# Attention and experts on one core: the choice on the tile count turned round, the small last tile in two banks, the gate products behind the first second product

## The chip, the cores and the metric

The kernel runs on one core of one Trainium2 chip. The metric is the device time of one execution in microseconds (us), as the median of several runs. Engines are named as in the profile: PE (TensorE products), PEld (its weight loads), DVE (VectorE), ACT (ScalarE), POOL (GpSimd), SP (SyncE, which issues most of the transfers).

## What is computed

Causal attention over 4 batches, 12 heads, 448 rows and a head width of 64 gives 1792 tokens of width 768. Each token then goes to one of 8 experts, the one with the largest cosine logit, and the expert's output is scaled by the gate:

```python
logits = xn @ en.T / tau
expert_idx = np.argmax(logits, axis=1)
gate_w = probs[np.arange(N), expert_idx]
for e in range(E):
    mask = expert_idx == e
    h = np.maximum(x[mask] @ w1[e], 0.0)
    out[mask] = gate_w[mask, None] * (h @ w2[e])
```

How many tokens an expert gets is only known on the chip.

## The kernel before

The first part is the attention. A list written out by hand (`ORDER`, lines 39 to 107) sets the order of its steps on every engine; it also holds the first expert tile (tile 0) up to most of its second product. The tokens are sorted by expert into tiles of at most 128 rows, each tile for one expert. With eight experts there are 13 to 21 tiles (`NT` is 21, `TMIN` is 14); the number is read from the chip into a register `nt` (line 1060). In the profiled execution there are 18 tiles, 0 to 17.

`body(t)` (line 969) does one tile: the first product of tile t (`product1`), the copies of its result by ACT (`hiddens`), the turning of the next tile's tokens (`turn_x`, line 631, transposes on PE), the gather of tile t+3 by POOL (line 568), then `turned_h` (line 742), which runs the second product of tile t-1 with the transposes of tile t's hidden values put among it, then `split_h` and `finish(t - 1)`: ACT scales the left half by the gate (line 797), DVE the right half (line 800), and POOL writes the rows out with an indirect transfer (line 818). Splitting the next weights into a high and a low part (`split_w`, lines 966 and 967) and loading the ones after them (`loads`, line 954) stand in between. `last(t)` (line 1003) does the second product of the very last tile and its `finish`.

Every product exists in several forms, of which a branch on the chip takes one per tile (`either`, `branch`, lines 580 to 607): *whole* for up to 128 rows (three products for each step of the sum, lines 705 to 707), *small* for up to 64 rows (two, lines 714 and 715) and, from tile 14 on, *tiny* for up to 32 rows (`tiny_product`, line 717). `tiny_product` puts four quarters of the columns on four groups of 32 partitions, all in the accumulator `acc[0]`; in `finish` ACT then scales quarters 0 and 1 (line 809) and DVE quarters 2 and 3 (line 810). Tile 17 is tiny.

Tiles 1 to 13 always exist. From tile 14 on, `rest(t)` (line 1066) chooses on `nt`. The code is nested: behind the choice comes the code of `body(t)`, then all that follows it, and only behind everything the code of `last(t - 1)`. So the code of `last(17)` stands behind that of tiles 18, 19 and 20, which this execution does not run.

```python
with tc.If(nt > t) as c:
    body(t)
    rest(t + 1)
hs[t - 1] = keep
with c.Else():
    last(t - 1)
```

The gate of each token is found by DVE, ACT and POOL (`gate_parts`, lines 1010 to 1035) while PE works on tile 1. `gates()` (line 1048) then brings the gates into the order of the tiles with 16 products on PE and three small operations on DVE; it stands in `body(1)` ahead of `turned_h`. `upper()` (line 1037, in `body(2)`) moves the gates to other partitions with products and two DVE copies, for the small and tiny forms.

PSUM has eight banks. In this part banks 0 and 1 hold the first product (`acc1`, and the second product of the last tile), banks 6 and 7 the second product (`acc2`), and banks 2 to 5 go round in `pt_ring` for transposes and gates.

Each engine runs its own instructions in the order of the code; which one waits for which is set by semaphores.

Of the kernel before, what the change touches and what calls it, by code (L numbers as in the profile page):

```python
# [20 lines left out]
DM, E, F = 768, 8, 1024  # L21
# [7 lines left out]
KD, KF = DM // P, F // P  # L29
# [5 lines left out]
QR = 32  # L35
NQ = P // QR
# [94 lines left out]
def attn_moe(tc, qk, vv, emb, tau, w1, w2, out):  # L131

    nc = tc.nc
    v, g, ac, pe, sy = nc.vector, nc.gpsimd, nc.scalar, nc.tensor, nc.sync
    with ExitStack() as ctx:
# [7 lines left out]
        def T(name, shape, d=F32, parts=CP):  # L143
            return kp.tile([parts] + shape, d, name=name)

        def cut(a, parts, *dims, at=0):

            n = 1
            for d in dims:
                n *= d  # L150
            a = a[:parts, at : at + n]
            if len(dims) == 1:
                return a
            names = "abcd"[: len(dims)]
            return a.rearrange(f"p ({' '.join(names)}) -> p {' '.join(names)}", **dict(zip(names, dims)))
# [59 lines left out]
        r2, xt0, r1 = cut(fa, P, KF, DM), cut(fa, P, DM, at=W), cut(fa, P, KD, F, at=W + DM)  # L215
        at = 2 * W + DM
        hh1, obs, xt1, hh0 = (cut(fa, P, n, at=at + o) for n, o in ((F, 0), (DM, F), (DM, F + DM), (F, F + 2 * DM)))
# [13 lines left out]
        xt_ring = Ring(xt0, xt1)  # L231
# [51 lines left out]
        gt, gu, gq = T("gt", [NT], parts=P), T("gu", [NT], parts=P), T("gq", [NT], parts=P)  # L283
        hq, xq = T("hq", [KF, QR], parts=P), en.rearrange("p k r -> p k r")
# [279 lines left out]
        xs, hs, hb = {}, {}, {}  # L564
# [37 lines left out]
        def either(t, engine, small_, whole_, light_=None, tiny_=None):  # L602

            if t < 2:
                whole_()
            else:
                branch(few[t][engine], small_, whole_, light_, tiny_ if t >= TMIN else None)
# [109 lines left out]
        def tiny_product(acc, x, w, nk, n):  # L717

            for k in range(nk):
                for q in range(NQ):  # L720
                    pe.matmul(acc[0][QR * q : QR * q + QR, :n], x[:, k], w[:, k, n * q : n * q + n], start=k == 0,
                              stop=k == nk - 1, tile_position=(0, QR * q), skip_group_check=True)

        few = [None] * NT

        def product1(t, acc):
            either(t, ET.PE, lambda: small_product(acc, xs[t][1], h1, l1, range(KD), KD, 512),
                   lambda: product(acc, *xs[t][1:], h1, l1, range(KD), (0, KD - 1), 512),
                   tiny_=lambda: tiny_product(acc, xq, r1, KD, F // NQ))

        def product2(t, acc):
            def small_():
# [9 lines left out]
        def turned_h(t, acc, ks):  # L742


            pf[t] = [cut(pt_ring.next(), P, 4, P) for a in range(2)]
            hs[t] = (hb[t], th_ring.next(), tl_ring.next())

            n = 3 if t > 1 else 1

            def among(f):  # L750
                f(ks[:-n])
                turn_h(t)
                f(ks[-n:])

            def whole_(k):
                product(acc, *hs[t - 1][1:], h2, l2, k, (K0[0], K0[-1]) if t == 1 else (0, KF - 1), 384)

            either(t - 1, ET.PE, lambda: among(lambda k: small_product(acc, hs[t - 1][1], h2, l2, k, KF, 384)),
                   lambda: among(whole_))
# [19 lines left out]
        acc2 = [bo[:, :384], bx[:, :384]]  # L779

        def finish(t, acc, ends):
            ob = xt_ring.next() if ends else obs

            def half(j):
                return ob[:, 384 * j : 384 * j + 384]

            def low(j):
                return hb[t][0:64, 384 * j : 384 * j + 384]

            def small_a(j):  # L790
                ac.activation(low(j), acc[j][64:128], AF.Copy, scale=gu[64:128, t : t + 1])

            def small_v(j):
                v.scalar_tensor_tensor(half(j)[0:64], acc[j][0:64], gt[0:64, t : t + 1], low(j), op0=ALU.mult, op1=ALU.add)

            def whole_a():
                ac.activation(half(0), acc[0], AF.Copy, scale=gt[:, t : t + 1])

            def whole_v():
                v.tensor_scalar(half(1), acc[1], gt[:, t : t + 1], None, ALU.mult)  # L800

            def quarters(qs, f):
                n = DM // NQ
                for q in qs:
                    rows = slice(QR * q, QR * q + QR)
                    f(ob[0:QR, n * q : n * q + n], acc[0][rows, :n], gq[rows, t : t + 1])

            def tiny_():
                quarters((0, 1), lambda o, x, s: ac.activation(o, x, AF.Copy, scale=s))
                quarters((2, 3), lambda o, x, s: v.tensor_scalar(o, x, s, None, ALU.mult))  # L810

            if ends and t > 1:
                branch(load_few(t, [ET.DVE, ET.Activation]), lambda: [f(j) for j in range(2) for f in (small_a, small_v)],
                       lambda: (whole_a(), whole_v()), tiny_=tiny_ if t >= TMIN else None)
            else:
                either(t, ET.Activation, lambda: [small_a(j) for j in range(2)], whole_a)
                either(t, ET.DVE, lambda: [small_v(j) for j in range(2)], whole_v)
            g.indirect_dma_start(out=out, out_offset=IndirectOffsetOnAxis(ap=isx[:, t : t + 1], axis=0), in_=ob,  # L818
                                 in_offset=None, bounds_check=N - 1, oob_is_err=False)
# [121 lines left out]
        for token in ORDER.split():  # L941
            name, p = token.split(".")
            pairs, f = steps[name]
# [24 lines left out]

        def body(t):
            product1(t, acc1)  # L970
            if t == 2:
                upper()
            elif t == 1:
                hidden(t, acc1, 0)
                hidden(t, acc1, 1)
            if t + 1 < NT:
                with tc.If(cc[t + 1] == 1):  # L977
                    split_w(r1, h1, l1, range(KD))
                loads(t + 2, 1)
            if t > 1:  # L980
                hiddens(t, acc1)
            if t + 1 < NT:
                few[t + 1] = {e: load_few(t + 1, [e]) for e in (ET.PE, ET.DVE, ET.Activation)}
            if t + 1 < NT:
                next_x(t + 1, turn_x(t + 1))
            if t + 3 < NT:
                gather(t + 3)
            if t == 1:
                gates()
            turn_light(t)  # L990
            ks = K0[GE:] if t == 1 else list(range(KF))
            turned_h(t, acc2, ks)
            if t > 1:
                with tc.If(cc[t] == 1):  # L994
                    split_w(r2, h2, l2, range(6))
            split_h(t)
            finish(t - 1, acc2, False)
            if t > 1:
                with tc.If(cc[t] == 1):  # L999
                    split_w(r2, h2, l2, range(6, KF))  # L1000
            loads(t + 1, 2)

        def last(t):
            acc = [a[:, :384] for a in acc1]
            product2(t, acc)
            finish(t, acc, True)
# [30 lines left out]
        def upper():  # L1037

            b = pt_ring.next()
            f, fq = b[:, :NT], b[:, NT : 2 * NT]  # L1040
            pe.matmul(f[64:128], idt[:, 0:64], gt, start=True, stop=True, tile_position=(0, 64), skip_group_check=True)
            v.tensor_copy(gu[64:128], f[64:128])
            for q in range(NQ):
                pe.matmul(fq[QR * q : QR * q + QR], idt[:, 0:QR], gt, start=True, stop=True, tile_position=(0, QR * q),
                          skip_group_check=True)
            v.tensor_copy(gq, fq)

        def gates():
            tg = cut(pt_ring.next(), P, 3, NT)
            for c in range(NCH):  # L1050
                pe.matmul(tg, M1[:, c], Mg[:, c], start=c == 0, stop=c == NCH - 1)
            v.tensor_copy(gt, tg[:, 2])
            v.scalar_tensor_tensor(gt, gt, 2.0 ** -12, tg[:, 1], op0=ALU.mult, op1=ALU.add)
            v.scalar_tensor_tensor(gt, gt, 2.0 ** -12, tg[:, 0], op0=ALU.mult, op1=ALU.add)
# [5 lines left out]
        nt = val(2 * NT, NT, [ET.SP, ET.Activation, ET.DVE, ET.PE, ET.Pool])  # L1060
        for t in range(1, TMIN):
            body(t)
            if t == 1:
                loads(2, 2)

        def rest(t):
            if t == NT:
                last(NT - 1)
                return
            keep = hs[t - 1]  # L1070
            with tc.If(nt > t) as c:  # L1071
                body(t)
                rest(t + 1)
            hs[t - 1] = keep
            with c.Else():
                last(t - 1)

        rest(TMIN)

# [34 lines left out]
```

## Time and profile before

| | |
|---|---|
| median of 3 runs | 505.75 us (505.46 to 508.03) |
| the profiled execution, its own time | 504.5 us |
| span of the profiled execution, first to last instruction | 502.7 us |
| busy: PE, DVE, ACT, POOL | 96%, 66%, 64%, 14% of the span |
| instruction transfers | 41 of 0.67 MB together on queue 8, 50 of 0.41 MB on queue 14 |
| weight transfers in all | 72.38 MB on queue 1 |

Times in the views are counted from the first instruction of the span. A matmul's start is measured, its end is modelled, so the next one may begin before the end that is shown. A row of a timeline gives start, duration, engine, line, operation, output and inputs, and in brackets how long the engine had been idle and what ended that. A q behind an engine (PEldq) is its sequencer: it reads the code, takes branches, and fills the engine's queue ahead of the engine. Queue 8 carries the code of PE, queue 14 that of the other engines.

### The profile page before, as it was taken

What the parts mean: (1) busy time and instruction counts of PE and PEld (TensorE: products, weight loads), DVE (VectorE), ACT (ScalarE), POOL (GpSimd) and SP (SyncE); (2) the same over time, 40 slices, a digit from 0 to 9 for tenths busy, and PEclk for the clock granted to TensorE, in tenths of its full rate; (3) what the DMA queues carried; (4) which work ended last, traced back from release to release, by engine and by line L of the source; (5) the groups of instructions that cost most, each with busy time, mean ns of one, the idle gap of its engine ahead of it and who ended that gap; (6) DMA issues with size and microseconds to landing.
All of it is one profiled execution on the core that took longest, in us unless ns stands there. A gap on an engine that the chain in (4) does not pass through costs nothing. (4 is left out here: it accounts for less than half of the span.)

```text
span 502.7 us, 10651 instructions
## 1 busy us (share of the span) xinstructions
PE 484.6 (96%) x3180; PEld 384.1 (76%) x3180; DVE 334.0 (66%) x939; ACT 323.9 (64%) x795; POOL 69.7 (14%) x89
## 2 busy tenths in 40 slices
PE   8999999999999998999999999999999999999992
PEld 5656566666666566888899888999889889888981
DVE  4766585766758659862577886873989367478431
ACT  5999999999999994641135965354938352161530
POOL 2000000000000262221002121111202210110111
PEclk9999999999999999999999999999999999999998
DMA  8232453173136862312167871649577701827871
GB/s 257 62 107 82 132 173 111 57 217 113 57 101 196 319 236 90 95 32 64 57 260 289 341 262 68 249 151 398 185 282 288 250 34 33 309 94 279 308 264 37
DMA packets 27371, 87.23 MB, mean 174 GB/s; under 512 B 2694, under 2 KB 3142, under 8 KB 27280
## 3 DMA queue, kind: packets, MB, share of 16 engines
q1 hardware_dynamic: 24160, 72.38, 41.3%
q0 software_dynamic: 3120, 13.77, 7.5%
q8 instruction: 41, 0.67, 0.6%
q14 instruction: 50, 0.41, 0.2%
HBM read 144.33 MB, written 12.58 MB: 312 GB/s over the span
## 5 line engine op out<-in xcount | busy, mean ns | idle before, releaser
L383 ACT ACTIVATE aq<-aq,mx 112x112 f32<-112x112 f32 (+3 forms) x192 | 99.8, 525 | 4.1 <-DVE mx L378 4.1
L378 DVE CUSTOM_DVE_ANT_0 aq<-bank,ar 112x112 f32<-112x112 f32 (+1 forms) x192 | 76.1, 442 | 30.2 <-PE bank L373 29.9
L401 PE MATMUL bank<-idt,aq 112*112 112x112 f32 x480 | 62.5, 266 | 1.2 <-DVE ap L406 0.5
L401 PEld LDWEIGHTS bank<-idt,aq 112*112 112x112 f32 x480 | 46.6, 133 | 19.8 <-ACT ap L406 6.8
L373 PE MATMUL bank<-ak 64*112 64x112 f32 (+3 forms) x384 | 56.2, 416 | 1.0 <-DVE mx L378 0.8
L764 ACT COPY fa<-bank 128x512 f32<-128x512 f32 x28 | 15.2, 588 | 59.9 <-PE bank L705 41.9
L406 ACT COPY ap<-bank 112x336 f32<-112x336 f32 (+2 forms) x118 | 50.7, 458 | 3.4 <-PE bank L401 1.8
L414 PE MATMUL bank<-ap 112*64 112x448 f32 (+3 forms) x384 | 51.7, 407 | 0.0
L663 DVE STREAM_TRANSPOSE turned<-fa 32x256 f32<-32x256 f32 x112 | 48.8, 436 | 1.5
L818 POOL DMA_INDIRECT out_dram<-fa,isx x18 | 24.1, 1341 | 180.7 <-DVEq L999 55.8
L414 PEld LDWEIGHTS bank<-ap 112*64 112x64 f32 x384 | 25.0, 136 | 30.0 <-issue 18.6
L967 DVE TENSOR_TENSOR wl<-fa,wh 128x1024 fp32r<-128x1024 f32 x36 | 41.5, 1220 | 3.1 <-PE bank L706 1.6
L966 ACT CAST wh<-fa 128x1024 fp32r<-128x1024 f32 x36 | 34.9, 1047 | 3.5 <-PE bank L707 1.6
L383 ACT ACTIVATION_READ_ACCUMULATOR aq<-aq,mx 112x1 f32 x192 | 37.1, 193 | 0.0
L373 PEld LDWEIGHTS bank<-ak 64*112 64x112 f32 x384 | 27.0, 173 | 13.0 <-issue 3.1
L568 POOL DMA_INDIRECT fa<-xd,ig x21 | 23.2, 1104 | 75.3 <-PE bank L636 52.9
L705 PE MATMUL bank<-wh,akr 128*128 128x512 f32 x84 | 32.9, 391 | 0.0
L707 PE MATMUL bank<-wh,akr 128*128 128x512 f32 x84 | 32.9, 391 | 0.0
L707 PE MATMUL bank<-wh,apr 128*128 128x512 f32 x84 | 32.9, 391 | 0.0
L706 PE MATMUL bank<-wl,akr 128*128 128x512 f32 x84 | 32.8, 390 | 0.0
L706 PE MATMUL bank<-wl,aor 128*128 128x512 f32 x84 | 32.8, 390 | 0.0
L705 PE MATMUL bank<-wh,aor 128*128 128x512 f32 x84 | 32.8, 390 | 0.0
(311 smaller groups left out, 1023.3 us busy)
## 6 DMA issues: line engine op xcount, KB each, us to landing
fa<-in_w_dram SPq DMA_DIRECT2D x76, 768.0 KB
fa<-in_w_dram SPq DMA_DIRECT2D x54, 1024.0 KB
ak<-in_qk_dram SPq DMA_DIRECT2D x24, 448.0 KB
ap<-in_vv_dram SPq DMA_DIRECT2D x24, 224.0 KB
xd<-fa SPq DMA_DIRECT2D x3, 1344.0 KB
fa<-in_w_dram SPq DMA_DIRECT2D x6, 512.0 KB
xd<-fa SPq DMA_DIRECT2D x1, 1120.0 KB
fa<-xd,ig POOLq DMA_INDIRECT x21, 6.3
```

The lines of the kernel that those rows point to most:

```text
L373: pe.matmul(o, raws[p % 4][rows, 0, CP * i : CP * i + CP], raws[p % 4][rows, 1, :n], start=True, stop=True, tile_position=(D * h, 0), skip ...
L378: v.tensor_tensor_reduce(out=Ps[p % 2][i, h], in0=st.pop(("sp", p, i, h)), in1=mask[i], scale=-0.125, scalar=3e38, op0=ALU.add, op1=ALU.mi ...
L383: ac.activation(x, x, AF.Exp, bias=mxs[p % 3][:, h, i : i + 1], scale=-1.0, accum_out=sums[p % 3][:, h, i : i + 1])
L401: pe.transpose(t[:, x, c], Ps[p % 2][i, h][:, c * CP : c * CP + CP], idt[:CP, :CP])
L406: (ac.copy if q == "A" and (p, n) not in ONV else v.tensor_copy)(o, st.pop(("pt", p, n)))
L414: pe.matmul(bo[64 * h : 64 * h + 64, CP * c : S], vts[p % 4][:, c, 64 * h : 64 * h + 64], PTs[p % 2][:, h, 4 * c : 3 * c + NC], start=c == ...
L663: v.transpose(xk[32 * j : 32 * j + 32, :, q : q + 32], blocks[q : q + 32, :, j])
L705: pe.matmul(acc[j], xh[:, k], wh[k][:, o], start=k == ends[0], stop=False)
L706: pe.matmul(acc[j], xh[:, k], wl[k][:, o], start=False, stop=False)
L707: pe.matmul(acc[j], xl[:, k], wh[k][:, o], start=False, stop=k == ends[1])
L966: ac.copy(h[k], r[:, k])
L967: v.tensor_tensor(l[k], r[:, k], h[k], op=ALU.subtract)
```

## The change

`gates()` moves behind `turned_h` in `body(1)`. In `upper()` the DVE copy of the first product moves behind the four other products. `tiny_product` spreads its four quarters over the accumulators that it is given: the second product gives two, so that quarters 0 and 1 lie in one bank and 2 and 3 in another, while the first product gives one, as before. `rest(t)` asks the opposite question, so that the code of `last(t - 1)` stands right behind the choice, and the code of `body(t)` behind that. As `last` is now written down before the gathers of later tiles, its output buffer is taken from the ring of token buffers without turning the ring; for tile 17 that is the other one of the two.

```diff
             for k in range(nk):
                 for q in range(NQ):
-                    pe.matmul(acc[0][QR * q : QR * q + QR, :n], x[:, k], w[:, k, n * q : n * q + n], start=k == 0,
-                              stop=k == nk - 1, tile_position=(0, QR * q), skip_group_check=True)
+                    pe.matmul(acc[q * len(acc) // NQ][QR * q : QR * q + QR, :n], x[:, k], w[:, k, n * q : n * q + n],
+                              start=k == 0, stop=k == nk - 1, tile_position=(0, QR * q), skip_group_check=True)
...
-                   tiny_=lambda: tiny_product(acc, xq, r1, KD, F // NQ))
+                   tiny_=lambda: tiny_product(acc[:1], xq, r1, KD, F // NQ))
...
         def finish(t, acc, ends):
-            ob = xt_ring.next() if ends else obs
+            ob = xt_ring.tiles[xt_ring.n % 2] if ends else obs
...
-                    f(ob[0:QR, n * q : n * q + n], acc[0][rows, :n], gq[rows, t : t + 1])
+                    f(ob[0:QR, n * q : n * q + n], acc[q // 2][rows, :n], gq[rows, t : t + 1])
...
-            if t == 1:
-                gates()
             turn_light(t)
             ks = K0[GE:] if t == 1 else list(range(KF))
             turned_h(t, acc2, ks)
+            if t == 1:
+                gates()
...
             pe.matmul(f[64:128], idt[:, 0:64], gt, start=True, stop=True, tile_position=(0, 64), skip_group_check=True)
-            v.tensor_copy(gu[64:128], f[64:128])
             for q in range(NQ):
                 pe.matmul(fq[QR * q : QR * q + QR], idt[:, 0:QR], gt, start=True, stop=True, tile_position=(0, QR * q),
                           skip_group_check=True)
+            v.tensor_copy(gu[64:128], f[64:128])
             v.tensor_copy(gq, fq)
...
-            keep = hs[t - 1]
-            with tc.If(nt > t) as c:
+            with tc.If(nt <= t) as c:
+                last(t - 1)
+            with c.Else():
                 body(t)
                 rest(t + 1)
-            hs[t - 1] = keep
-            with c.Else():
-                last(t - 1)
```

## Rows read from the trace of the kernel before

**Rows 1.** The page: busy time of each engine, share of the span, instructions.

```profile
PE 484.6 (96%) x3180; PEld 384.1 (76%) x3180; DVE 334.0 (66%) x939; ACT 323.9 (64%) x795; POOL 69.7 (14%) x89
```

**Rows 2.** Timelines of PE, DVE and POOL at the end, from 489 us on.

```profile
489.60 0.34 PE L707 MATMUL bank<-apr,aqr 128*128 128x384 f32 x1
491.08 3.33 PE L721 MATMUL bank<-fa,hq 128*32 128x192 f32 x64 [1.14 <-DVE fa L800]
...
490.44 0.62 DVE L800 TENSOR_SCALAR fa<-bank,gt 128x384 f32<-128x384 f32 x1 [5.72 <-ACTq L999]
495.44 0.87 DVE L810 TENSOR_SCALAR fa<-bank,gq 32x192 f32<-32x192 f32 x2 [4.39 <-ACT fa L809]
...
491.87 1.02 POOL L818 DMA_INDIRECT out_dram<-fa,isx  x1 [8.99 <-DVEq L999]
497.46 1.00 POOL L818 DMA_INDIRECT out_dram<-fa,isx  x1 [4.58 <-POOLq L1071]
```

**Rows 3.** Output writes of POOL, 491 to 503 us: time until the rows have landed.

```profile
DMA to landing us min/median/max: 2.8/3.8/4.8
```

**Rows 4.** Timeline of PE around the gate products, 219 to 222 us.

```profile
219.57 0.82 PE L636 MATMUL bank<-idt,fa 128*128 128x128 f32 x6
221.23 0.67 PE L1051 MATMUL bank<-Mg,turned 112*128 112x63 f16 x16 [0.85 <-POOL Mg L1035]
```

**Rows 5.** Timeline of DVE behind the gate products, 221 to 226 us.

```profile
224.13 1.29 DVE L691 SCALAR_TENSOR_TENSOR apr<-bank,aor 128x512 fp32r<-128x512 f32 x2 [0.71 <-ACT aor L693]
```

**Rows 6.** Timeline of PE in `upper`, 232.7 to 234.8 us.

```profile
233.10 0.29 PE L1041 MATMUL bank<-gt,idt 128*64 128x21 f32 x2
233.67 0.26 PE L1044 MATMUL bank<-gt,idt 128*32 128x21 f32 x8 [0.28 <-DVE gu L1042]
234.05 0.85 PE L636 MATMUL bank<-idt,fa 128*128 128x128 f32 x6
```

**Rows 7.** The choice on `nt` on PE's sequencer (count: ns min/median/max, start), tiles 16 and 18.

```profile
L1071 PEldq COMPARE_BRANCH  x1: 70/70/70, 456.3 to 456.3; - x1
L1071 PEldq COMPARE_BRANCH  x1: 3719/3719/3719, 486.7 to 486.7; - x1
```

**Rows 8.** Timeline of PE: the first product behind the choice of tile 16.

```profile
459.40 0.39 PE L705 MATMUL bank<-wh,akr 128*128 128x512 f32 x1
```

**Rows 9.** Code of PE: its queue from 14.5 to 191.4 us, instructions executed meanwhile.

```profile
q8 instruction: 11, 0.18, 0.4%
...
14.88:191.59 176.71, 174.72 (x1405) 109.81 (x1402) 119.80 (x515) 170.62 (x543) 15.89 (x28) 1.00 0.44 145
```

**Rows 10.** Code of PE: windows 487.5 to 487.6 and 487 to 491 us.

```profile
q8 instruction: 1, 0.02, 78.7%
...
q8 instruction: 1, 0.02, 2.0%
```

**Rows 11.** Branches on PE's sequencer: line 597 at 479.7, line 653 at 435.5 and 453.1 us.

```profile
L597 PEldq COMPARE_BRANCH  x1: 1283/1283/1283, 479.7 to 479.7; - x1
...
L653 PEldq COMPARE_BRANCH  x1: 327/327/327, 435.5 to 435.5; - x1
...
L653 PEldq COMPARE_BRANCH  x1: 209/209/209, 453.1 to 453.1; - x1
```

**Rows 12.** Code of PE: windows 478.6 to 478.7 and 459.9 to 460.1 us.

```profile
q8 instruction: 1, 0.02, 59.2%
...
q8 instruction: 1, 0.02, 31.9%
```

**Rows 13.** Windows behind the choices of tiles 15, 16, 17: last figures clock, DMA share, GB/s.

```profile
438.70:440.00 1.30, 1.30 (x8) 1.30 (x9) 1.26 (x3) 0.00 (x0) 0.00 (x0) 1.00 0.95 384
440.00:443.00 3.00, 3.00 (x18) 2.78 (x17) 2.23 (x6) 0.59 (x1) 0.00 (x0) 1.00 0.05 17
456.29:460.00 3.71, 3.71 (x21) 3.62 (x22) 3.58 (x9) 0.00 (x0) 0.00 (x0) 1.00 0.93 351
474.36:475.00 0.64, 0.64 (x6) 0.64 (x5) 0.64 (x2) 0.64 (x2) 0.00 (x0) 1.00 0.04 14
```

## The prediction, made from the kernel before alone

> **What bounds the kernel now.** I read the page first: PE is busy for 96% of the span [rows 1], so the time is PE's stream, its few stops, and what follows its last product. The timeline of PE shows those stops from tile 1 on: one before the gate products [rows 4], two in `upper` [rows 6], one before the last product [rows 2]. Each of the four parts of the change aims at one of them or at what comes behind the last product. The other views say who is late next.
>
> **Gates.** The last transpose before them would have been followed 0.11 us after it was issued (six transposes are issued over 0.54 us from 219.57, so the next at 220.22); the gate products start at 221.23 because POOL is late with its part [rows 4]. Behind `turned_h` they meet data that has been ready for over 2 us, so PE gains 1.0 us; the idle time alone is 0.85, the lower bound. The 16 products still run, so nothing above 1.0 is to be had. The three DVE operations that read them now wait until about 224, and `split_h` of DVE (line 691), which ran from 224.13 [rows 5], queues behind them, as do the scalings of `finish(0)` on both engines and the write of POOL: each about 0.6 us later. The first PE work that needs what they write is the second product of tile 2, behind the transposes of 234.05 [rows 6], some 8 us later; that covers it, and without this cover 0.6 us of the gain would go. `gates` issues no transfer, so no queue of SP or POOL is passed.
>
> **Upper.** The second group of products waits for the first DVE copy, and the transposes behind for that group: issued at 233.10, 233.67, 234.05 [rows 6]. Without the wait the ten products are issued over some 0.2 us and the transposes follow by about 233.4: 0.6 us gained. The bounds are the idle time that the row names, 0.28, and the 0.95 us from 233.10 to 234.05 less the 0.2 of issuing, 0.75. The copies are needed by later tiles only.
>
> **Two banks.** DVE starts its two quarters when ACT has finished its own (the row names ACT's line 809) and takes 0.87 us [rows 2]. In another bank it can run beside ACT: 0.9 us less. But DVE is done at 496.31 and POOL's last write starts at 497.46. The write before it starts at 491.87 and lands 4.8 us later [rows 2, 3], at 496.67; POOL's last write starts 0.8 us after that, the distance that it also kept from DVE's scaling (ended 491.06) at the write before. So the last write waits for the landing of the write before, not for DVE. I cost this part at nothing: it is covered by a slack of 0.35 us that only grows. The other buffer, whose gather is older, costs nothing for the same reason.
>
> **The last part beside its tile.** Before, PE's choice for tile 18 is a jump to code far behind: it takes 3.72 us, where that of tile 16 takes 0.07 [rows 7]. PE's queue holds work for the first 3.1 us: at tile 16 the choice falls at 456.3 and the first product behind it starts at 459.40 [rows 7, 8]. At the far jump 4.4 us pass until 491.08 [rows 2], so it costs PE 1.3 us. After the change this jump is gone, and the last product starts 1.3 us earlier. That too is worth nothing, since the last write waits for the landing of the write before, whose own time does not change.
>
> The other side is that tiles 14 to 17 now take a jump over `last(13)` to `last(16)`. On POOL, SP, ACT and DVE that skips 10 to 25 instructions and I cost it at nothing: they idle behind PE for microseconds per tile. On PE it is long. I counted PE's instructions through the code: a whole or small product counts two (a load and a product), a tiny one four (32 of them are 64 products in [rows 2]), a wait or branch one. `last` has 298 of them from tile 14 on; the skipped small form of the next first product adds 52, the skipped tiny form 99. So PE's sequencer passes some 450 instructions within a microsecond, where it now passes 150.
>
> What that costs depends on how the code arrives. From 14.88 to 191.59 us, with almost no jumps, 11 transfers brought 0.18 MB for 2807 products and loads [rows 9]: a block of 16 KB holds about 256 instructions. At the far jump one block comes, starting at 487.5, and none until 491 [rows 10]: one block at a time, the next only after its predecessor is entered. A branch at 479.7 of 1.28 us lasts until 2.4 us after the block fetched at 478.6 [rows 11, 12]: it stood waiting for a block already asked for. So after entering a block, the one behind it is not there for several us. The jump of 7 instructions at 435.5 takes 0.33 us, where the same one a tile later takes 0.21 [rows 11]; I take that as a block's edge, which fits the 94 instructions within which the branch at 479.7 puts one. Counted from there, the choice of tile 14 stands 162 instructions before an edge and skips 317: it ends in the next block, already there. Those of tiles 15, 16 and 17 stand about 50, 62 and 74 before an edge and skip 450, 450 and 352: each crosses two edges and **must wait for a block**. My count would have to be off by ten one way or fifty the other before one of them drops out.
>
> The price of such a stop of length L is L + 0.7 - 3.1 = L - 2.4, where 0.7 us are the branches and waits behind the jump (4.4 - 3.72). The lower end of L is where the block is there: no cost; I exclude a gain, as PE is never idle at these choices now. The nearest row is the far jump: block asked for at 486.7, begun at 487.5, jump over at 490.4: L 3.7, cost 1.3. The upper end is a block that queues behind weights: at tile 16 a new block is entered just behind the choice at 456.3, and its transfer starts only at 459.9 [rows 12] with the DMA engines 0.93 busy in between [rows 13]. With 2.5 us from start to release (between 2.4 and 2.9 above) that is L 6.2, cost 3.8.
>
> For tile 15 the transfers are busy until 440.0, 1.3 us behind the choice, then quiet [rows 13]: L 1.3 + 2.5 = 3.8, cost 1.4. For tile 16 I take the upper end, 3.8. For tile 17 they are quiet when the choice is made, 0.04 [rows 13]: as at the far jump, 1.3. Together 6.5 us, between 0 and 11.4.
>
> One page of the Trainium skill bears on this, "Runtime: NRT & Kernel Launch", section "Instruction fetch mechanics". It says that a taken branch to code outside a window of two pages of 256 instructions forces a fetch before work goes on; the block size and the single block ahead agree with the rows. The same section gives PE's code memory as 2048 instructions; if those were filled ahead, a skip of 450 would cost nothing, which is the first rival below, but the rows show one block at a time.
>
> **Sum.** -1.0 - 0.6 + 6.5 = +4.9 us. The profiled execution took 504.5 us of its own time, 1.8 over its span and 1.25 below the median of 505.75; I add to the median: **510.65 us**. A measurement of this kernel can tell about 0.5%, 2.5 us, from no change.
>
> **Rivals.** (1) *The code is there*: all blocks skipped into have been fetched, each jump costs 0.07 us. Then only the gains of gates and upper remain: 505.75 - 1.6 = 504.15, no slower. For it: every jump within the tiles now is nearly free; against it the 1.28 us branch [rows 11]. It decides from a stop below 2.4 us, which PE's queue covers. (2) *All three blocks queue behind weights*, as at tile 16: 11.4 - 1.6 = +9.8, 515.5. For it: weights are moving in most of these stretches; against it [rows 13] for tiles 15 and 17. (3) *The last write does not wait for the landing before*: then it follows the scalings, and the earlier last product and the two banks count; DVE would be done at 494.1 (496.31 less 0.9 and 1.3) instead of the landing's 496.67, 2.55 us, and without stops that gives 501.6. Against it: the 0.8 us fit and the order of writes to one tensor is untouched. A stop is also milder in the forecast's own case if all three find quiet transfers: 3.9 - 1.6 = +2.3, 508.05.
>
> **How the numbers follow.** Forecast (three stops of whatever length between those ends) 0.66, rival 1 0.20, rival 2 0.08, rival 3 0.06. The forecast's own range is 508 to 513.5. Rival 1 belongs inside the range, with 0.3 us for its uncertain gains: 503.8; at the upper side I stop at 514.5, short of rival 2. Slower by over 0.5% (above 508.3): most of the forecast and rival 2, 0.60. Within: the mild end of the forecast and nearly all of rival 1, 0.27. Faster (below 503.2): rival 3 and a rival 1 with a better landing, 0.13.
>
> **What would show it.** In the changed profile PE should run without a stop from tile 1's transposes to its second product, and through `upper`. The choices of tiles 15, 16, 17 or the branch right behind each should last 3 to 6 us on PE's sequencer, with a block of code landing just before, and PE should idle over a microsecond behind each; tile 14 should not. DVE's quarters should run beside ACT's, and POOL's last write should still start 0.8 us after the landing of the one before. I am wrong if those branches stay below half a microsecond or PE does not idle behind them, or if the last write follows the scalings.

## The result and the profile after

| | before | after |
|---|---|---|
| median of 6 runs each | 505.68 us (505.13 to 508.03) | 511.51 us (509.73 to 512.76) |
| the profiled execution, its own time | 504.5 us | 512.76 us |
| its span | 502.7 us | 511.0 us |

The changed kernel takes 1.0108 times as long, with a 95% interval of 1.0079 to 1.0136: slower, with 5.8 us between the medians. The profiled execution of after is the slowest of its six, that of before is shorter than any of its six, so their spans differ by 8.3 us; what makes up the rest is shown below.

**What went as planned.** The timeline of PE at the gates and in `upper`, after (it answers to [rows 4] and [rows 6]):

```profile
223.14 0.34 PE L707 MATMUL bank<-arr,aqr 128*128 128x384 f32 x1
223.32 0.68 PE L1051 MATMUL bank<-Mg,turned 112*128 112x63 f16 x16
223.83 0.47 PE L705 MATMUL bank<-wh,akr 128*128 128x512 f32 x1
...
232.21 0.29 PE L1041 MATMUL bank<-gt,idt 128*64 128x21 f32 x2
232.43 0.26 PE L1043 MATMUL bank<-gt,idt 128*32 128x21 f32 x8
232.62 0.87 PE L636 MATMUL bank<-idt,fa 128*128 128x128 f32 x6
```

No bracket stands behind any of them: PE waits nowhere. The first product of tile 2, the last row of the first part, began at 224.80 before, so 0.97 us are gained there (0.88 at the product behind it, 224.15 for 225.03). In `upper` the products start 0.89 ahead of before (232.21 for 233.10) and the transposes 1.43 ahead (232.62 for 234.05): 0.54 us more. The lead at the second product behind them is 1.40 us, and up to 431 us it stays within 0.02 of that.

**What went wrong.** The branches of PE's sequencer at the choices (line 1070) and right behind them (line 597), after (they answer to [rows 7]; columns as there: count, ns, start):

```profile
L1070 PEldq COMPARE_BRANCH  x1: 423/423/423, 419.7 to 419.7; - x1
L1070 PEldq COMPARE_BRANCH  x1: 428/428/428, 437.3 to 437.3; - x1
L597 PEldq COMPARE_BRANCH  x1: 3535/3535/3535, 437.8 to 437.8; - x1
L1070 PEldq COMPARE_BRANCH  x1: 322/322/322, 456.3 to 456.3; - x1
L597 PEldq COMPARE_BRANCH  x1: 5665/5665/5665, 456.7 to 456.7; - x1
L1070 PEldq COMPARE_BRANCH  x1: 320/320/320, 479.2 to 479.2; - x1
L597 PEldq COMPARE_BRANCH  x1: 3268/3268/3268, 479.6 to 479.6; - x1
L597 PEldq COMPARE_BRANCH  x1: 3334/3334/3334, 485.3 to 485.3; - x1
L1070 PEldq COMPARE_BRANCH  x1: 72/72/72, 495.8 to 495.8; - x1
```

The five choices are those of tiles 14 to 18. That of tile 14 is followed by no long branch; those of 15, 16 and 17 are, by 3.5, 5.7 and 3.3 us. The choice of tile 18, the far jump of before [rows 7], now takes 72 ns. The fourth long branch, at 485.3, stands inside tile 17, where the sequencer skips the small form of the second product; the prediction did not have it. The code that these waits are for, after, two of four windows (459.9 to 460.1 and 480.2 to 480.4 us; packets, MB, and share of 16 engines' time; the other two, from 438.9 and 486.0 on, show one transfer each as well):

```profile
q8 instruction: 1, 0.02, 29.0%
...
q8 instruction: 1, 0.02, 35.8%
```

One block starts in each of the four, at 438.98, 459.95, 480.29 and 486.02. The branches end at 441.35, 462.37, 482.86 and 488.58, so 2.4 to 2.6 us later each time. What differs is how long the transfer takes to begin: 1.2 and 0.7 us after the branch at tiles 15 and 17, but 3.25 us at 456.7, where weights are moving (DMA share 0.96). The fourth begins 0.8 us after its branch, though weights are moving there too (0.82). It may have been asked for earlier: counted from the end of the stop before it (482.86) it begins 3.16 us later, at a share of 0.94. Behind the stops of tiles 15 and 16 the next block begins 0.8 us after the stop's end where the transfers are quiet (442.14), and 2.7 us after it where they are not (465.04, share 0.78). No view shows when a block is asked for. What PE does meanwhile is in its timeline, after:

```profile
440.26 0.34 PE L707 MATMUL bank<-apr 128*128 128x384 f32 x1
441.80 0.47 PE L705 MATMUL bank<-wh,aor 128*128 128x512 f32 x1 [1.20 <-DVEq L994]
...
459.26 0.34 PE L707 MATMUL bank<-apr,aqr 128*128 128x384 f32 x1
462.82 0.77 PE L705 MATMUL bank<-wh,akr 128*128 128x512 f32 x1 [3.23 <-ACT aor L693]
...
482.14 0.34 PE L707 MATMUL bank<-apr 128*128 128x384 f32 x1
483.16 1.07 PE L721 MATMUL bank<-fa,en 128*32 128x256 f32 x16 [0.68 <-DVE apr L967]
...
485.88 0.88 PE L636 MATMUL bank<-idt,fa 128*128 128x128 f32 x6
488.75 0.41 PE L705 MATMUL bank<-arr 128*128 128x384 f32 x1 [1.99 <-DVEq L665]
```

The brackets name DVE three times and ACT once as what ended the idle time. For ACT the kernel before refutes it: there the same operation (line 693) ran from 461.65 to 462.71, and the first product of tile 16 had started at 459.40 [rows 8], without it. The products behind the four stops start 0.45, 0.45, 0.30 and 0.17 us after the end of the long branch in front of them; a stop of the sequencer does not stand in PE's brackets, and the view of its branches has to be laid beside them.

Two more things differ in this execution. The first is the granted clock. Three windows, after. Behind the span and its length stand the busy times of PE, PEld, DVE, ACT and POOL, then clock, DMA share, GB/s.

```profile
456.70:459.90 3.20, 2.90 (x17) 2.58 (x15) 3.08 (x8) 0.00 (x0) 0.00 (x0) 1.00 0.96 364
...
462.23:465.64 3.41, 2.82 (x7) 2.27 (x8) 1.75 (x2) 0.98 (x2) 0.24 (x1) 0.50 0.79 252
...
489.53:492.95 3.42, 3.42 (x12) 3.42 (x12) 0.04 (x1) 0.00 (x0) 0.00 (x0) 0.50 0.89 326
```

Around two of the stops the clock falls to 0.50, the lower of its two levels (1.2 instead of 2.4 GHz), for 3.4 us. The first product of tile 16 then takes 9.63 us (462.82 to 472.45) where it took 8.20, and the stretch from 488.75 to the last whole product, at 498.79, takes 10.04 us, where before needed 8.48 (481.12 to 489.60). Together 3.0 us.

The second is the end. Timelines of DVE, ACT and POOL, after (they answer to [rows 2]):

```profile
499.63 0.62 DVE L800 TENSOR_SCALAR fa<-bank,gt 128x384 f32<-128x384 f32 x1 [10.06 <-PE bank L721]
502.62 0.86 DVE L810 TENSOR_SCALAR fa<-bank,gq 32x192 f32<-32x192 f32 x2 [2.38 <-PE bank L721]
...
502.56 0.85 ACT L809 ACTIVATE fa<-bank,gq 32x192 f32<-32x192 f32 x2 [3.02 <-PE bank L721]
...
501.06 1.02 POOL L818 DMA_INDIRECT out_dram<-fa,isx  x1 [12.53 <-DVEq L999]
505.80 1.00 POOL L818 DMA_INDIRECT out_dram<-fa,isx  x1 [3.72 <-POOLq L1070]
```

DVE's quarters run beside ACT's and are done at 503.48. The write of 501.06 has landed 3.93 us later, when POOL's sequencer goes on (504.99), and the last write starts 0.81 after that: it waits for the landing, as forecast. The time until the rows have landed, for the last two output writes of POOL, after (it answers to [rows 3]; the longest is this write):

```profile
DMA to landing us min/median/max: 2.5/3.2/3.9
```

This landing took 3.93, not the 4.8 of [rows 3], and so the end came 0.85 nearer to the last whole product than before.

**The span adds up.** Gates and `upper` -1.40. The stops, each as the distance between the two starts above less the 0.17 us that such products follow one another: +1.37 (tile 15), +3.39 (16), +0.85 (17), and +2.04 in front of the product of 488.75 (2.87 us behind the row before it, 0.83 in the kernel before). The clock +3.0, the landing -0.85. Together +8.4; the spans differ by 8.3.

### The profile page after: what moved, and what is told of

Read it like the earlier page. It is cut to its first block, busy times and chain, and to the rows that moved or that the text cites. A ratio compares the mean times of both kernels' runs of the same rounds, so it can differ in the third digit from the quotient of the medians.

```text
span 511.0 us, 10649 instructions
## 1 busy us (share of the span) xinstructions
PE 487.6 (95%) x3180; PEld 386.5 (76%) x3180; DVE 334.3 (65%) x939; ACT 324.3 (63%) x795; POOL 70.9 (14%) x89
## 5 line engine op out<-in xcount | busy, mean ns | idle before, releaser
L705 PE MATMUL bank<-wh,akr 128*128 128x512 f32 x84 | 33.7, 401 | 3.2 <-ACT aor L693 3.2
L707 PE MATMUL bank<-wh,akr 128*128 128x512 f32 x84 | 33.3, 397 | 0.0
```

Source lines behind the costliest of these rows:

```text
L705: pe.matmul(acc[j], xh[:, k], wh[k][:, o], start=k == ends[0], stop=False)
L707: pe.matmul(acc[j], xl[:, k], wh[k][:, o], start=False, stop=k == ends[1])
```

## The experiments

All ran beside the kernel before, whose median was 505.14 us (20 runs) next to the first four and 505.15 (29 runs) next to the others. `v` is DVE; "after" is the changed kernel.

**The choice restored, all else as in after.**

```diff
-            with tc.If(nt <= t) as c:
-                last(t - 1)
-            with c.Else():
+            keep = hs[t - 1]
+            with tc.If(nt > t) as c:
                 body(t)
                 rest(t + 1)
+            hs[t - 1] = keep
+            with c.Else():
+                last(t - 1)
```

`finish` also takes its buffer by turning the ring again.

> The change without its turned choice: gates, upper and the two banks as changed, the code of last() far behind again. Code theory (PE waits for blocks of its own code after the jumps over last): the three stops go, 505.7 - 1.4 = 504.3 us, no idle time of PE over 0.6 us between 210 us and the last product, and the 3.7 us jump at tile 18 is back. Rival (the time was lost to the moved gates or to the two banks): stays near 511.5 us.

502.74 us (12 runs), ratio 0.9955 (0.9935 to 0.9974). All of the loss is gone, so gates, `upper` and banks cost nothing, and the kernel is the fastest complete one of this study: the three other parts are worth 2.4 us, a microsecond more than the 1.4 of gates and `upper`. Its far jump, on PE's sequencer, took longer than that of before [rows 7]:

```profile
L1071 PEldq COMPARE_BRANCH  x1: 4624/4624/4624, 485.3 to 485.3; - x1
```

and PE idled behind it, in its timeline:

```profile
490.66 0.65 PE L721 MATMUL bank<-fa,hq 128*32 128x192 f32 x9 [2.04 <-SPq L1071]
```

**The choice alone, all else as before.**

```diff
-            ob = xt_ring.next() if ends else obs
+            ob = xt_ring.tiles[xt_ring.n % 2] if ends else obs
...
-            keep = hs[t - 1]
-            with tc.If(nt > t) as c:
+            with tc.If(nt <= t) as c:
+                last(t - 1)
+            with c.Else():
                 body(t)
                 rest(t + 1)
-            hs[t - 1] = keep
-            with c.Else():
-                last(t - 1)
```

> The kernel before with the turned choice alone. Code theory: the same stops on PE's sequencer right behind the choices of tiles 15, 16 and 17 (3.3 to 5.7 us each) and none at tile 14, and no gain from gates and upper: 511.5 + 1.4 = 512.9 us. Rival (moved gates or banks cost the time): 505.7 us.

511.98 us (4 runs), ratio 1.0152 (1.0113 to 1.0191). The choice alone brings the whole loss. Its long branches on PE's sequencer:

```profile
L597 PEldq COMPARE_BRANCH  x1: 3725/3725/3725, 439.6 to 439.6; - x1
L597 PEldq COMPARE_BRANCH  x1: 5732/5732/5732, 458.7 to 458.7; - x1
L597 PEldq COMPARE_BRANCH  x1: 3128/3128/3128, 480.3 to 480.3; - x1
L597 PEldq COMPARE_BRANCH  x1: 2969/2969/2969, 485.8 to 485.8; - x1
```

PE's timeline behind the second of them, and the window around it (columns as above):

```profile
464.89 0.47 PE L705 MATMUL bank<-wh,akr 128*128 128x512 f32 x1 [3.29 <-ACT aor L693]
```

```profile
460.00:465.00 5.00, 1.71 (x11) 1.42 (x10) 3.65 (x9) 1.31 (x2) 0.00 (x0) 1.00 0.52 194
```

The same four stops in the same places. But here the clock stayed at 1.00 through an idle time of 3.29 us, and the execution, at 511.80 us, was the quickest of the four. Measured as above, its stops come to 1.55, 3.47, 0.71 and 1.67 us, together 7.4, and its span (510.1 us) is 7.4 us longer than that of before; what else differs, some 0.4 us each way, cancels. So the stops alone carry the loss, and in the profiled execution of after the clock came on top.

**A short part in the skipped place.** In after, the code of `last(13)` to `last(16)`, which this input never runs, is left out; one small operation of DVE stands for each.

```diff
             with tc.If(nt <= t) as c:
-                last(t - 1)
+                if t < 18:
+                    v.memset(apart, 0.0)
+                else:
+                    last(t - 1)
```

> The changed kernel, choice turned, but last(13) to last(16), which this execution never runs, are left out of the code (one small DVE operation stands in each place), so that the jump skips 4 instead of 299 instructions of PE. Code theory: the jumps are as short as those within a tile now, no stop of over 0.5 us behind the choices of tiles 14 to 17, 505.7 - 1.4 - 0.9 = 503.4 us. Rival (the opposite question itself costs, by waits that stand at the start of the other branch, or the next weights come late): the stops stay, near 511.5 us.

502.40 us (9 runs), ratio 0.9943 (0.9921 to 0.9965). The choice is the turned one, and yet nothing is lost. The choices of tiles 15 to 17 on PE's sequencer, and the longest branch from there to the last product, which before had as well, at 1.28 us [rows 11]:

```profile
L1070 PEldq COMPARE_BRANCH  x1: 213/213/213, 437.3 to 437.3; - x1
L1070 PEldq COMPARE_BRANCH  x1: 203/203/203, 454.9 to 454.9; - x1
L1070 PEldq COMPARE_BRANCH  x1: 208/208/208, 473.0 to 473.0; - x1
...
L597 PEldq COMPARE_BRANCH  x1: 1041/1041/1041, 478.3 to 478.3; - x1
```

So it is not the direction of the question, nor the order of the branches, but the code that lies between the choice and its target.

**A long part in the skipped place.** In after, the parts skipped at tiles 14 to 17 get the second product three times; none of this code runs.

```diff
             with tc.If(nt <= t) as c:
+                if t < 18:
+                    for _ in range(2):
+                        product2(t - 1, [x[:, :384] for x in acc1])
                 last(t - 1)
```

> The changed kernel with the second product written three times in last(13) to last(16), none of which is run: the jump skips 491 instructions at tile 14 and 885 at tiles 15, 16 and 17. Code theory: a block's wait now stands at the choice itself and at tile 14 too, where there was none; at tiles 15 and 16 the skip behind the choice crosses a further edge, so two blocks in a row, 6 to 9 us; in all 6 to 10 us more than the changed kernel, 517 to 522 us. A theory in which the time grows with the instructions skipped (three times as many) gives 511.5 + 2 x 7 = 525 us or more; one in which the skipped code does not matter, 511.5 us.

521.69 us (4 runs), ratio 1.0316 (1.0277 to 1.0355). Its long branches on PE's sequencer, tiles 14 to 16:

```profile
L1070 PEldq COMPARE_BRANCH  x1: 3760/3760/3760, 419.4 to 419.4; - x1
L1070 PEldq COMPARE_BRANCH  x1: 3677/3677/3677, 438.8 to 438.8; - x1
L593 PEldq COMPARE_BRANCH  x1: 3038/3038/3038, 442.8 to 442.8; - x1
L1070 PEldq COMPARE_BRANCH  x1: 6267/6267/6267, 463.1 to 463.1; - x1
L593 PEldq COMPARE_BRANCH  x1: 5043/5043/5043, 469.8 to 469.8; - x1
```

Three times as much to skip (at tiles 15 and 16) does not make a jump three times as long. Now the jump itself waits, at tile 14 too, for as long as a single stop did; where the next branch crosses an edge again (tiles 15 and 16), a second stop follows within 0.4 us, and there PE idles 4.25 and 8.56 us, since its queue covers such a time only once. So it goes by blocks entered, each with its wait, and not by instructions skipped.

**Only the last of the four parts short** (in after; `last(16)`, not run here, is left out, so the choice of tile 17 has little to skip).

```diff
             with tc.If(nt <= t) as c:
-                last(t - 1)
+                if t == 17:
+                    v.memset(apart, 0.0)
+                else:
+                    last(t - 1)
```

> The changed kernel with last(16) alone left out of the code (it is not run here), so that only the choice of tile 17 has a short jump. Code theory: the stops behind the choices of tiles 15 and 16 stay as they are (3.5 and 5.7 us on PE's sequencer); the stop of 3.3 us behind tile 17's choice and the later one of 3.3 us in the same tile, at the skipped small form of the second product, go or fall below 1.5 us: 511.5 - 0.9 - 2.0 = 508.6 us, 507 to 509 with the clock. If the later stop is a cost of its own in tile 17 and not an effect of the jump: 510.6 us.

509.35 us (10 runs, 507.66 to 512.13), ratio 1.0078 (1.0057 to 1.0099), 0.35 us above the expected stretch, which had allowed for the clock; in its profiled execution (509.87 us) the clock fell to 0.50 for 3.4 us behind the stop of tile 16. The median lies between the two figures that the expectation gives, so the trace has to decide. Branches on PE's sequencer behind the choices of tiles 15, 16 and 17, with that of 17 itself:

```profile
L597 PEldq COMPARE_BRANCH  x1: 3545/3545/3545, 438.6 to 438.6; - x1
L597 PEldq COMPARE_BRANCH  x1: 5912/5912/5912, 457.6 to 457.6; - x1
L1070 PEldq COMPARE_BRANCH  x1: 213/213/213, 480.6 to 480.6; - x1
L597 PEldq COMPARE_BRANCH  x1: 887/887/887, 485.9 to 485.9; - x1
```

The stops of tiles 15 and 16 stay, both of tile 17 are gone: the one at its choice and the later one, which so belongs to the jump. How the jump makes the later one was not tried by itself (the edit also moves the edges of all code behind it).

**The banks, in three places.** All three change only how many banks the tiny product uses. In the kernel with the choice restored, back to one bank:

```diff
-                    pe.matmul(acc[q * len(acc) // NQ][QR * q : QR * q + QR, :n], ...
+                    pe.matmul(acc[0][QR * q : QR * q + QR, :n], ...
...
-                    f(ob[0:QR, n * q : n * q + n], acc[q // 2][rows, :n], gq[rows, t : t + 1])
+                    f(ob[0:QR, n * q : n * q + n], acc[0][rows, :n], gq[rows, t : t + 1])
```

> e1_choice_back with the small last tile in one bank again. In e1_choice_back the write before the last landed at 494.5 and DVE ended at 494.96, with the last write 0.8 us after DVE: there the scalings are later than the landing. Theory (the banks count where the far jump makes the last product late and the landing is quick): DVE ends 0.9 us later and the last write follows it, 502.7 + 0.9 = 503.6 us. The step of the prediction (the banks are worth nothing, the last write waits for the landing): 502.7 us.

503.77 us (12 runs), ratio 0.9968 (0.9949 to 0.9987): about 1 us of what the restored choice had is gone, so the banks count there. What is left is before with the moved gates and the changed `upper` alone, and it gains 1.38 us (505.15 less 503.77), the 1.40 that the trace of after shows for these two. The same edit in the kernel with the short parts:

> e3_short_last with the small last tile in one bank again. There the last product is early: DVE ended at 492.1 and the write before landed at 494.3. Both theories of e5: DVE ends near 493.0, still ahead of the landing, so no difference, 502.4 us. A theory in which the two banks save 0.9 us wherever they are: 503.3 us.

502.57 us (6 runs), ratio 0.9938 (0.9914 to 0.9963): no difference to 502.40, so here they don't. And the two banks added to before, the reverse of the diff and with no other part of the change:

> The kernel before with the two banks alone. In its profile the landing was 0.35 us later than DVE's end; its landing took 4.8 us, where e1, e2 and e3 show 4.0, 4.3 and 4.1. Theory of e5: with such a landing DVE's end is what the last write waits for by about 0.4 us, and the banks bring that: 505.1 - 0.4 = 504.7 us. The step of the prediction: 505.1 us, no change.

504.40 us (12 runs), ratio 0.9980 (0.9962 to 0.9998): a gain of 0.75 us.

In the timelines of DVE and POOL, the last scaling and the last write with the choice restored: first two banks, then one.

```profile
494.09 0.86 DVE L810 TENSOR_SCALAR fa<-bank,gq 32x192 f32<-32x192 f32 x2 [4.36 <-PE bank L721]
495.77 1.00 POOL L818 DMA_INDIRECT out_dram<-fa,isx  x1 [4.20 <-POOLq L1071]
```

```profile
495.33 0.87 DVE L810 TENSOR_SCALAR fa<-bank,gq 32x192 f32<-32x192 f32 x2 [5.01 <-ACT fa L809]
497.01 1.00 POOL L818 DMA_INDIRECT out_dram<-fa,isx  x1 [4.86 <-POOLq L1071]
```

In both the last write starts 0.81 us after DVE's end (494.95, 496.20), and 1.25 and 2.03 after the landing of the write before (494.52, 494.98): here it waits for DVE. POOL's sequencer shows it too, at line 818 with the choice restored and two banks (count: ns min/median/max, start; the 481 ns are the wait that begins at 494.5, when the landing is over):

```profile
L818 POOLq EVENT_SEMAPHORE  x3: 17/481/2959, 486.8 to 494.5; - x3
```

In before and in after that second wait takes 0.04 us. To compare kernels without their earlier parts I take the time from the start of DVE's scaling of tile 16 (line 800) to that of the last write:

| kernel (profiled execution) | far jump | banks | write lands after, us | line 800 to last write, us |
|---|---|---|---|---|
| before | yes | 1 | 4.8 | 7.02 |
| choice restored, one bank | yes | 1 | 3.84 | 7.30 |
| before with two banks | yes | 2 | 3.85 | 6.38 |
| choice restored | yes | 2 | 3.97 | 6.65 |
| short parts, one bank | no | 1 | 4.03 | 6.26 |
| short parts | no | 2 | 4.07 | 6.29 |
| after | no | 2 | 3.93 | 6.17 |

With the far jump a second bank takes 0.64 and 0.65 us off this distance; without the jump it takes nothing. The 0.64 is in part the shorter landing, as before's profiled execution waited for its 4.8 us; the 0.65 compares two executions that both waited for DVE.

## Why the prediction was right, and where its steps were not

Forecast were 510.65 us, 4.9 more than before; measured were 511.51 us, 5.8 more.

**The stops, the term that decided it, are shown.** They stand behind the choices of tiles 15, 16 and 17 and not 14, they come with the turned choice alone, go with it, and go with the code that is skipped though the choice stays. The rival "the code is there" falls with that. So does what the page "Runtime: NRT & Kernel Launch" of the Trainium skill would have given, had PE's 2048 instructions been filled ahead (section "Instruction fetch mechanics"). The trace agrees with the rule of the same section, that a taken branch to a page out of the window of two waits for that page: each of the three long branches behind the choices waits for one block.

**Their sizes.** Tile 15: 1.37 for 1.4. Tile 16: the long branch was 5.67 us where L was to be 6.2 with the jump in it (5.99 with the choice), cost 3.39 for 3.8; the block began 3.25 us after the branch, with weights moving, as the upper end had it. Tile 17: 0.85 for 1.3, and the idle time of PE there, 0.68, is under the microsecond that was to show it. The three together cost 5.6 where 6.5 was forecast, and the 2.5 us from the start of a transfer to the release held at 2.4 to 2.6.

**Missing: the later stop in tile 17**, 2.0 us. The step that failed is the count of crossings: it went through the choices only and not on through the branches behind them, as though after a stop the queue of PE and the block ahead were as full as before. They are not: the sequencer has just come out of a wait, and 2.4 us later it stands at a block that is not there (it began 3.16 us after that wait, with weights moving). The kernel with only the last of the four parts short shows that this stop goes with the jump; how the jump brings it about stays open.

**Missing: the clock**, 3.0 us in the profiled execution. The sum took idle time of PE as lost only while it lasts. The mean granted clocks of the six runs are 0.989 in the two slowest (512.70 and 512.76 us) and 0.991 or 0.992 in the other four; before's profiled execution had 0.996. How much it takes of the other runs is not shown: with the choice alone an execution at 0.990 took 511.84 us, 0.04 more than the one at 0.994.

**Gates** right: 0.97 for 1.0, of which 0.89 reached `upper`, with the rest covered as argued. **Upper** 0.54 in place for 0.6: the ten products took 0.41 us to issue (232.21 to 232.62), where "some 0.2" was put. 0.51 of it was left at the second product (1.40 less 0.89).

**"Two banks: nothing" was wrong as a rule and right for after.** It rested on a slack of 0.35 us that one execution showed, with a landing of 4.8 us. In the profiled executions of the nine other kernels the landing took 3.5 to 4.3 us. With the far jump, DVE is then done after the landing, the last write follows the scalings as in the third rival, and what shortens DVE's work counts: 0.75 us in before alone (505.15 less 504.40). With the choice restored the medians differ by 1.0 us, from two sessions; the distance in the trace says 0.65. That is also why the choice restored gains more than gates and `upper`. In after the far jump is gone, the last product comes early, and the landing is last: there the step held, and the last write kept its 0.8 us.

**"The far jump: nothing"** does not hold as a rule either. With one bank, the kernels with and without the jump differ by 1.2 us (503.77 with the choice restored, 502.57 with short parts). With two banks they differ by 0.34 us (502.74 and 502.40). That is little against the noise, but the table has 0.36 for it (6.65 less 6.29), and with the jump POOL still waits 0.4 us for DVE after the landing. So the second bank takes off most of what the far jump costs, and not all.

That the total came as near as 0.9 us is in part luck, because terms missed on both sides partly cancel: against 6.5 us of stops stood 5.6, 2.0 more for the stop not seen, a clock loss that varies, and a shorter landing.

## What to carry to other kernels

Before code is put between a choice and its target, count the instructions that the busiest engine's sequencer has to pass: in the traces here about 256 come at a time and one block is fetched ahead, so what is usually taken belongs right behind its choice, and the rare part far behind. When an engine idles behind a branch and the bracket names an engine that had its work done in the other kernel, lay the branches of the engine's own sequencer and the queue that carries its code beside it. A slack of a few tenths of a microsecond against the landing of a transfer is no cover until it has been seen in several executions.

## What was not expected of the hardware

The clock. In after it fell to 0.50 during an idle time of 3.23 us of PE, and again 0.8 us after one of 1.99 us had ended; in the kernel with long parts it fell for 6.8 and 10.2 us around idle times of 4.25 and 8.56; in the profiled execution of the choice alone it stayed at 1.00 through 3.29 us. What decides this was not settled. And one jump to the same far code took 3.72, 4.02, 4.00 and 4.62 us in four kernels (before, before with two banks, choice restored with one bank and with two), so a single profile gives such a price to within about a microsecond.
